# Weight conversions, block sums and one eviction placed elsewhere in the order of a fused attention and MLP kernel

## The chip, the cores and the metric

The kernel runs on one core of a Trainium2 chip. Five engines work side by side, each on its own list of instructions in order: PE (TensorE, matmul), DVE (VectorE), ACT (ScalarE), POOL (GpSimd) and SP (SyncE, which here only issues DMAs). The metric is the device time of one execution in microseconds (us). The kernel before takes 791.88 us, the median of five runs (791.40 to 792.34).

## The reference

Two blocks follow each other. The first is a cross attention between 512 tokens and 32 states, for 8 batches of 8 heads of width 64, read in both directions. The second is an MLP whose hidden layer is multiplied by its own cosine.

```python
scores = scale * np.matmul(x, state.transpose(0, 1, 3, 2))
a = softmax(scores)            # max taken off, sum + 1e-09
xread = np.matmul(a, state)
scores2 = scale * np.matmul(state, x.transpose(0, 1, 3, 2))
a2 = softmax(scores2)
sread = np.matmul(a2, x)
attn_out = np.concatenate([xread, sread], axis=2)
...
x = attn_out.transpose(0, 2, 1, 3).reshape(B * S, H * D)   # 8 x (512 + 32) rows of 512
h = x @ w_in                   # 512 x 2048
g = h * np.cos(h)
return g @ w_out               # 2048 x 512
```

The attention's inputs are float32. `w_in` and `w_out` are float64, so the kernel turns them into float32 from their bits.

## The kernel before, in words

**Steps and tiles.** The order of all instructions is written out by hand. The kernel walks through 144 tiles, one for each step of the loop at L838: 16 tiles for each of the 8 batches (one for each 128 of the 2048 hidden columns), and 16 more for the state rows. A step belongs to one tile t. `hidden(t)` (L466) computes the 128x512 pre-activation h on PE, from the attention weights `aT` and the product `sw` of the states with `w_in`. The gate then goes `gate` (L475, ACT: add a large number to round), `gate2` (L478, DVE: subtract), `gate3` (L483 and L484, ACT: Abs, then Sin) and `gate4` (L490, DVE: multiply by h, write a slot of `g_all`). There are two PSUM buffers for h, so the h of a tile waits for gate4 of the tile two before it.

**Output.** `output(t)` (L609) multiplies a finished tile with `w_out` on PE (L534). It comes three tiles later (`LAG`), four in the first 16 steps, at the end of a step. Batches are taken in pairs with a seven product scheme after Strassen, over the four blocks a11, a12, a21, a22 of `w_out`. A tile has a phase: 0 and 1 are the halves of the first batch of the pair, 2 and 3 those of the second. Phase 0 uses a11, phase 1 a12, phase 2 the block sum s1, phase 3 the sums s4 and s2. What is left over of a pair (`p7` with s3, `p4` with a22) is done while the next pair runs (`more`, L515). In phases 2 and 3 `sums` and `sums2` take differences of tiles (L496); in the first pair all of them on POOL.

**Block sums.** `blocks` (L822) computes half of a block sum in one POOL instruction (L823, 128x1024), at the step that `block_at` (L826) gives: s1 = a21 + a22, s2 = s1 - a11, s4 = a12 - s2, s3 = a11 - a21, where s3 overwrites a21.

**Weights.** 18 loads of float64 weights (L166) are fetched into three raw areas inside `g_all`. Loads 4, 5, 7, 8, 10 and 11 are parts of `w_in` from its second 512 columns on; 6 and 9 are a11, 12 and 13 a12, 14 and 16 a22, 15 and 17 a21. `convert(i, parts)` (L205) turns load i into float32 in six operations: "1" (L224) and "2" (L227) on ACT, "a", "b" and "c" (L231, L233, L236) on DVE, "d" (L241) on POOL. Part "f" fetches load i + 3 into the raw area that is now free, on SP's queue (L194). `conv_at` (L818) gives the step of "1" and "2"; the other parts come one step later. "2" writes one of two scratch areas by turns, which "d" reads.

**Attention of the next batch.** The batch after the current one is prepared between the steps, by the plan at L747: `tokens` and `scores` on PE, `max1`, `spread1`, `shift`, `max2`, `sums` and `norm1` on DVE, `exps` on ACT, then `turn` and `reads` on PE, and the four `products` of states and `w_in` (L316), each with an eviction to `sw` (L443) by ACT (`products_kept`) or DVE (`products_taken`). After the second `reads` of a batch the x of the next one is loaded on SP's queue (L289, L109, L112). In step 6 `states_kept` (L148, DVE) evicts the second half of the transposed states. `warm` (L708) issues matmuls whose result nobody uses.

**Inside a step** the order is: `hidden`, PE's parts of the plan, `gate`, `gate2`, the first parts of ACT and DVE, the parts "a" to "f" of the last conversion, "1" of the present one (or after gate4, where ACT has a first part), `gate3`, `gate4`, `sums`, the second parts, "2", the block sum, `sums2` and `output`. In step 3 four warm matmuls and the products of batch 0's second 512 columns are put in by hand, with their eviction, ahead of the first parts.

Of the kernel before, what the change touches and what calls it, by code (L numbers as in the profile page):

```python
# [12 lines left out]
ALU = mybir.AluOpType  # L13
# [10 lines left out]
def kernel(  # L24
# [47 lines left out]
    a11, a12 = w_out[:, 0, 0:NH], w_out[:, 0, NH:NF]  # L72
    a21, a22 = w_out[:, 1, 0:NH], w_out[:, 1, NH:NF]
    s1 = consts.tile([P, NH, HD], F32)
    s2 = consts.tile([P, NH, HD], F32)
    s3 = a21
    s4 = consts.tile([P, NH, HD], F32)
# [26 lines left out]
    def load_x(b):  # L104

        src = x[b].rearrange("h (c p) d -> p c h d", p=P)
        if b < 2:
            for h in range(H):
                nc.sync.dma_start(out=x_b[:, :, h], in_=src[:, :, h])  # L109
        else:  # L110
            for c in range(NC):
                nc.sync.dma_start(out=x_b[:, c], in_=src[:, c])  # L112
# [27 lines left out]
    def states(half, to):  # L140
        for i in range(4):
            nc.tensor.transpose(out=to[:, P * i:P * i + P],
                                in_=st[:, 4 * half + i, :], identity=ident)

    def states_kept(half, to):
        dst = slice(4 * half, 4 * half + 4)
        src = to.rearrange("p (b m) -> p b m", b=4)
        nc.vector.tensor_scalar(stT[:, dst], src, 1.0 / TWO_PI, None,  # L148
                                op0=ALU.mult)
# [30 lines left out]
    def fetch(n):  # L180
        nonlocal n_fetched
        while n_fetched < n:
            dst, src = loads[n_fetched]
            if f64:
                m, w = dst.shape[1:]

                at_, c0 = (n_fetched - 2) % 3, 0
                if n_fetched < 4:
                    at_, c0 = n_fetched // 2, n_fetched % 2 * 2 * m * w
                if n_fetched >= N_LOADS:  # L190
                    at_ = 3 + n_fetched - N_LOADS
                raw = raw_at[at_].bitcast(I32)[:, c0:c0 + 2 * m * w]
                raw = raw.rearrange("p (m f) -> p m f", m=m)
                nc.sync.dma_start(out=raw, in_=src.bitcast(I32))  # L194
                raws[n_fetched] = raw.rearrange("p m (f w) -> p m f w", w=2)
            else:
                nc.sync.dma_start(out=dst, in_=src)
            n_fetched += 1
# [6 lines left out]
    def convert(i, parts):  # L205

        for p in parts:  # L210
            if p == "f":
                if i not in (1, 2) and i + 3 < N_LOADS:
                    fetch(max(i + 4, 6))
            elif f64:
                convert_part(i, p)
# [32 lines left out]
    class Attention:  # L248
# [126 lines left out]
        def sums(self):  # L375
            self.reduce1([self.z1[:, j] for j in range(2)], ALU.add)
            self.inverse(self.m1 if self.b == 0 else self.i12)
# [73 lines left out]
    def part(b, name, *args):  # L451

        if b not in attn:
            attn[b] = Attention(b)
        getattr(attn[b], name)(*args)
        if (name, args) == ("reads", (1,)) and b + 1 < B:
            if b > 0:
                attn[b + 1] = Attention(b + 1)
                attn[b + 1].load_tokens()
            load_x(b + 1)  # L460
# [5 lines left out]
    def hidden(t):  # L466
        t.hp = hps.tile([P, S], F32, name="h")[:, 0:t.n]
        for i in range(t.kn):
            nc.tensor.matmul(out=t.hp, lhsT=t.lhs(i), rhs=t.rhs(i),  # L469
                             start=(i == 0), stop=(i == t.kn - 1))  # L470

    def gate(t):

        t.q = msb.tile([P, S], F32, name="q")[:, 0:t.n]
        nc.scalar.activation(t.q, t.hp, func=ACTF.Copy, bias=MAGIC)  # L475

    def gate2(t):
        nc.vector.scalar_tensor_tensor(out=t.q, in0=t.q, scalar=MAGIC,  # L478
                                       in1=t.hp, op0=ALU.subtract,
                                       op1=ALU.subtract)  # L480

    def gate3(t):
        nc.scalar.activation(t.q, t.q, func=ACTF.Abs)  # L483
        nc.scalar.activation(t.q, t.q, func=ACTF.Sin, bias=halfpi,  # L484
                             scale=-TWO_PI)

    def gate4(t):
        t.slot = g_free.pop(0)
        t.g = g_all[:, t.slot, 0:t.n]
        nc.vector.tensor_tensor(t.g, t.hp, t.q, op=ALU.mult)  # L490
# [7 lines left out]
    MAIN, SIDE = 0, 1  # L498
# [85 lines left out]
    def sums2(t):  # L584
        pr, i = t.pair, t.i
        if t.phase == 3:
            minus(pr, pr.b[1, i].g, pr.b[1, i].g, pr.b[0, i].g)
# [120 lines left out]
    def warm(n, to):  # L708

        for _ in range(n):  # L710
            nc.tensor.matmul(out=to, lhsT=zeros[:, 0:P], rhs=zeros, start=True,
                             stop=True)
# [34 lines left out]
    def plan(b):  # L747
# [68 lines left out]


    conv_at = {s: 4 + i for i, s in enumerate(  # L818
        (0, 1, 2, 3, 4, 5, 6, 7, 8, 10, 11, 12, 13, 14))}
    conv_at.update({B * NF + 5: N_LOADS, B * NF + 7: N_LOADS + 1})  # L820

    def blocks(op, out_, a, b, r):  # L822
        nc.gpsimd.tensor_tensor(out_[:, r], a[:, r], b[:, r], op=op)  # L823

    lo, hi = slice(0, NH // 2), slice(NH // 2, NH)
    block_at = {15: (ALU.add, s1, a21, a22, lo),  # L826
                17: (ALU.add, s1, a21, a22, hi),
                18: (ALU.subtract, s2, s1, a11, lo),
                19: (ALU.subtract, s2, s1, a11, hi),
                20: (ALU.subtract, s4, a12, s2, lo),  # L830
                21: (ALU.subtract, s4, a12, s2, hi),
                22: (ALU.subtract, s3, a11, a21, lo),
                23: (ALU.subtract, s3, a11, a21, hi)}
    LAG = 3

    line = []
# [1 line left out]
    for step, t in enumerate(all_tiles):  # L838
        s = step % NF
        if s == 0 and t.b < B:  # L840
            steps = plan(t.b)
        todo = [p[s] if t.b < B else [] for p in steps]

        def go(n):
            for p in todo[n]:
                part(*p)

        last, conv = conv_at.get(step - 1, -1), conv_at.get(step, -1)
        if step == B * NF + (0 if f64 else 8):
            fetch(N_LOADS + 2)  # L850
        if step == 4:
            warm(1, acc[MAIN][0])
        if step != 1:
            hidden(t)
        if step == 0:
            hidden(all_tiles[1])
            warm(3, acc[MAIN][0])
            gate(t)
            gate2(t)
            convert(3, "bcdf")  # L860
            convert(4, "1a")
            go(0)
        else:
            go(0)
            if step == 5:
                states(1, acc[SIDE][1])
            gate(t)
            gate2(t)
            if step == 3:
                warm(4, acc[MAIN][0])  # L870
                part(0, "products", 1, SIDE)
                part(0, "products_kept", 1, SIDE)
            go(1)
            go(3)
            if step == 1:
                convert(4, "bcdf")
            elif last >= 0:
                convert(last, "abcdf")
            if conv >= 0 and not todo[1]:
                convert(conv, "1")  # L880
        gate3(t)
        if later:
            later.pop(0)()
        gate4(t)
        if conv >= 0 and todo[1] and step > 0:
            convert(conv, "1")
        if t.pair is not None:
            sums(t)
        if step == 6:
            states_kept(1, acc[SIDE][1])  # L890
        go(2)
        if conv >= 0:
            convert(conv, "2")
        go(4)
        if step in block_at:
            blocks(*block_at[step])
        if t.pair is not None:
            sums2(t)
        while len(line) >= (LAG if step >= 2 * NH else LAG + 1):
            output(line.pop(0))  # L900
        line.append(t)
# [32 lines left out]
```

## Time and profile before

| | before |
|---|---|
| median of 5 runs | 791.88 us |
| the profiled execution's own time | 791.40 us |
| its span, first to last instruction | 789.6 us |
| PE busy | 766.6 us (97%), 2664 matmuls |
| DVE busy | 431.0 us (55%) |
| ACT busy | 390.3 us (49%) |
| POOL busy | 178.7 us (23%) |
| PE o L534, all forms (with `w_out`, with sums) | 236.4 and 177.3 us |
| PE h L469 (512 wide) | 241.6 us |
| POOL g_all L496 | 112.1 us, 80 times, 1422 ns each |
| POOL L241 on w_out | 23.9 us, 10 times, 2393 ns each |
| mean granted TensorE clock | 0.999 |

A page of the profile gives busy times by engine and by group of instructions; a group is a source line, an engine, and what it writes and reads (`o<-g_all,w_out`). A wait is put down to the engine and line that released it last. In the timeline a row has its start and its duration in us, engine, line, operation, output and inputs with shapes, and, in square brackets, how long the engine stood before it and what released it. A duration includes the end of an instruction that the next one on the same engine overlaps, so the distance from start to start is somewhat shorter than the duration. All instructions before about 200 us belong to the first pair of batches, with the weight conversions in its first 17 steps.

### The profile page before, as it was taken

Reading aid. Unit: us, or ns where it says so; the run is one execution under the profiler, and the core shown is the slowest. Engines: PE = TensorE matmul, PEld = TensorE weight load, DVE = VectorE, ACT = ScalarE, POOL = GpSimd, SP = SyncE. Lnnn points to the kernel's source line nnn. Section 1 sums busy time; section 2 is a strip of 40 time slices with the busy share of each in tenths; the row PEclk is TensorE's granted clock in tenths of the full one; section 3 lists DMA queues with packets and bytes.
Section 4 is the critical chain, followed back from the end, with each engine's and each line's share of the span. In section 5 each row is a group of like instructions: output and inputs, shape, how many; then the busy total and the mean of one; then the engine's idle time right before and its main releaser. Section 6 shows DMA issues by size and latency. Waiting matters only on the chain.

```text
span 789.6 us, 7555 instructions
## 1 busy us (share of the span) xinstructions
PE 766.6 (97%) x2664; PEld 340.4 (43%) x2664; DVE 431.0 (55%) x675; ACT 390.3 (49%) x626; POOL 178.7 (23%) x119
## 2 busy tenths in 40 slices
PE   8998899899999999999999999999999999999997
PEld 4442333344344344444444434434444444455554
DVE  5879887732564467744554467635553545431531
ACT  3877964644364445643473436443563445322222
POOL 3343359684000000451000000740000004610200
PEclk9999999999999999999999999999999999999999
DMA  8484361041010610150003410340100114000021
GB/s 239 160 244 182 126 141 28 0 88 20 0 27 13 107 27 14 30 104 0 15 14 54 80 27 6 53 76 0 27 1 0 27 27 117 17 0 15 14 41 40
DMA packets 161958, 43.49 MB, mean 55 GB/s; under 512 B 153921, under 2 KB 153921, under 8 KB 161921
## 3 DMA queue, kind: packets, MB, share of 16 engines
q1 hardware_dynamic: 161024, 42.49, 24.6%
q10 hardware_dynamic: 768, 0.39, 0.2%
q8 instruction: 21, 0.34, 0.2%
q0 software_dynamic: 128, 0.13, 0.1%
q14 instruction: 17, 0.13, 0.1%
HBM read 34.08 MB, written 8.91 MB: 54 GB/s over the span
## 4 chain that ended last, share of the span: by engine, by line
PE 80%; ACT 9%; DVE 8%; issue 1%; DMA 1%; POOL 1%; SPq 0%; ACTq 0%; DVEq 0%; POOLq 0%
PE o L534 44%; PE h L469 26%; PE at L316 4%; PE o L654 3%; PE at L406 2%; DVE q L478 1%; ACT q L483 1%; ACT q L484 1%; DVE g_all L490 1%; ACT s L227 1%; ACT q L475 1%; DVE xT L336 1%; ACT xT L362 1%; DVE aT L383 1%; PE o L316 1%
## 5 line engine op out<-in xcount | busy, mean ns | idle before, releaser
L469 PE MATMUL h<-aT,sw 128*128 128x512 f32 x512 | 241.6, 594 | 12.5 <-DVE g_all L490 10.3
L534 PE MATMUL o<-g_all,w_out 128*128 128x512 f32 x512 | 236.4, 598 | 1.2 <-POOL w_out L241 1.2
L496 POOL TENSOR_TENSOR g_all<-g_all 128x512 f32<-128x512 f32 x80 | 112.1, 1422 | 450.8 <-DVE g_all L490 447.2
L475 ACT ACTIVATE q<-h 128x512 f32<-128x512 f32 (+1 forms) x144 | 82.3, 571 | 261.0 <-PE h L469 260.9
L478 DVE SCALAR_TENSOR_TENSOR q<-q,h 128x512 f32<-128x512 f32 (+1 forms) x144 | 94.2, 654 | 207.2 <-ACT q L475 207.1
L534 PE MATMUL o<-g_all,s 128*128 128x512 f32 x384 | 177.3, 598 | 0.0
L490 DVE TENSOR_TENSOR g_all<-h,q 128x512 f32<-128x512 f32 (+1 forms) x144 | 94.8, 658 | 124.4 <-ACT q L484 118.2
L469 PEld LDWEIGHTS h<-aT,sw 128*128 128x128 f32 x512 | 96.3, 190 | 137.4 <-issue 109.2
L534 PEld LDWEIGHTS o<-g_all,w_out 128*128 128x128 f32 x512 | 94.0, 190 | 125.5 <-issue 118.4
L483 ACT ACTIVATE q<-q 128x512 f32<-128x512 f32 (+1 forms) x144 | 87.8, 610 | 96.3 <-DVE q L478 96.3
L534 PEld LDWEIGHTS o<-g_all,s 128*128 128x128 f32 x384 | 70.8, 190 | 91.7 <-issue 87.3
L484 ACT ACTIVATE q<-q,halfpi 128x512 f32<-128x512 f32 (+1 forms) x144 | 100.9, 700 | 4.5
L241 POOL TENSOR_TENSOR w_out<-w_out,s 128x1024 int32<-128x1024 int32 x10 | 23.9, 2393 | 79.5 <-DVE w_out L236 79.5
L496 DVE TENSOR_TENSOR g_all<-g_all 128x512 f32<-128x512 f32 x48 | 33.2, 692 | 1.6
L443 ACT COPY sw<-at 128x512 f32<-128x512 f32 x50 | 26.8, 590 | 9.0 <-PE at L316 9.0
L469 PE MATMUL h<-sT,w_in 128*128 128x256 f32 x128 | 30.2, 379 | 0.0
L654 PE MATMUL o<-w_out,g_all 128*128 128x512 f32 x64 | 29.6, 592 | 0.0
L469 PEld LDWEIGHTS h<-sT,w_in 128*128 128x128 f32 x128 | 24.3, 190 | 10.1 <-issue 6.2
L316 PE MATMUL at<-w_in,stT 64*32 64x512 f32 x400 | 27.2, 601 | 0.0
L241 POOL TENSOR_TENSOR w_in<-w_in,s 128x1024 int32<-128x1024 int32 (+1 forms) x10 | 19.6, 1964 | 32.1 <-DVE w_in L236 18.5
L540 DVE SCALAR_TENSOR_TENSOR held<-o,held 128x512 f32<-128x512 f32 x40 | 25.3, 676 | 2.3 <-PE o L534 2.3
L561 DVE STREAM_TRANSPOSE ot<-held 128x512 f32<-128x512 f32 x32 | 22.2, 692 | 0.0
(83 smaller groups left out, 445.0 us busy)
## 6 DMA issues: line engine op xcount, KB each, us to landing
out_dram<-ot SPq DMA_DIRECT2D x132, 64.0 KB, 2.0
g_all<-in_moe_w_out_dram SPq DMA_DIRECT2D x8, 1024.0 KB, 4.9
g_all<-in_moe_w_in_dram SPq DMA_DIRECT2D x6, 1024.0 KB, 5.2
xT<-in_x_dram SPq DMA_DIRECT2D x96, 64.0 KB, 2.3
x_b<-in_x_dram SPq DMA_DIRECT2D x24, 256.0 KB, 4.7
x_b<-in_x_dram SPq DMA_DIRECT2D x16, 128.0 KB, 4.0
g_all<-in_moe_w_in_dram SPq DMA_DIRECT2D x4, 512.0 KB, 6.0
x_b<-in_moe_w_out_dram SPq DMA_DIRECT2D x1, 1024.0 KB, 5.9
```

What stands on the lines that cost most here:

```text
L241: nc.gpsimd.tensor_tensor(bits, bits, e.bitcast(I32), op=ALU.add)
L316: nc.tensor.matmul(out=(to or at)[j][Ns * k:Ns * k + Ns, 0:n], lhsT=w[D * j:D * j + D, self.b, Ns * k:Ns * k + Ns], rhs=r(slice(D * j, D * ...
L443: (copy or nc.scalar.copy)(sw_of[self.b, nt][:, j, c0:c1], to[j][:, 0:c1 - c0])
L469: nc.tensor.matmul(out=t.hp, lhsT=t.lhs(i), rhs=t.rhs(i), start=(i == 0), stop=(i == t.kn - 1))
L475: nc.scalar.activation(t.q, t.hp, func=ACTF.Copy, bias=MAGIC)
L478: nc.vector.scalar_tensor_tensor(out=t.q, in0=t.q, scalar=MAGIC, in1=t.hp, op0=ALU.subtract, op1=ALU.subtract)
L483: nc.scalar.activation(t.q, t.q, func=ACTF.Abs)
L484: nc.scalar.activation(t.q, t.q, func=ACTF.Sin, bias=halfpi, scale=-TWO_PI)
L490: nc.vector.tensor_tensor(t.g, t.hp, t.q, op=ALU.mult)
L496: engine.tensor_tensor(out, a, b, op=ALU.subtract)
L534: nc.tensor.matmul(out=acc[bank][ch], lhsT=w[:, i, P * ch:P * ch + P], rhs=g.g, start=(i == 0), stop=(i == NH - 1))
L654: nc.tensor.matmul(out=acc[MAIN][i], lhsT=t.g[:, P * i:P * i + P], rhs=w_out[:, :, t.f, :], start=(t.n_th == 0), stop=(t.n_th == NF - 1))
```

## The change

Three places in the hand-written order change; the operations themselves, their number and their sizes stay as they are.

Conversions 10 to 17 go to later steps: 10 from step 6 to 7, 11 from 7 to 8, 12 from 8 to 10, 13 from 10 to 11, 14 from 11 to 12, 15 from 12 to 13, 16 from 13 to 14, 17 from 14 to 15. Their DVE and POOL parts and their fetches follow one step behind, as before. Steps without "1" and "2" are now 6 and 9 (9 and 15 before).

The six halves of s1, s2 and s4 go one step later each, and the two of s3 from steps 22 and 23 to 32 and 33, which are the first two of the second pair.

The ACT eviction of the products in step 3 goes from before the first parts to behind `gate3`, that is behind that step's conversion part "1", Abs and Sin.

```diff
     conv_at = {s: 4 + i for i, s in enumerate(
-        (0, 1, 2, 3, 4, 5, 6, 7, 8, 10, 11, 12, 13, 14))}
+        (0, 1, 2, 3, 4, 5, 7, 8, 10, 11, 12, 13, 14, 15))}
...
-    block_at = {15: (ALU.add, s1, a21, a22, lo),
-                17: (ALU.add, s1, a21, a22, hi),
-                18: (ALU.subtract, s2, s1, a11, lo),
-                19: (ALU.subtract, s2, s1, a11, hi),
-                20: (ALU.subtract, s4, a12, s2, lo),
-                21: (ALU.subtract, s4, a12, s2, hi),
-                22: (ALU.subtract, s3, a11, a21, lo),
-                23: (ALU.subtract, s3, a11, a21, hi)}
+    block_at = {16: (ALU.add, s1, a21, a22, lo),
+                18: (ALU.add, s1, a21, a22, hi),
+                19: (ALU.subtract, s2, s1, a11, lo),
+                20: (ALU.subtract, s2, s1, a11, hi),
+                21: (ALU.subtract, s4, a12, s2, lo),
+                22: (ALU.subtract, s4, a12, s2, hi),
+                32: (ALU.subtract, s3, a11, a21, lo),
+                33: (ALU.subtract, s3, a11, a21, hi)}
...
             if step == 3:
                 warm(4, acc[MAIN][0])
                 part(0, "products", 1, SIDE)
-                part(0, "products_kept", 1, SIDE)
             go(1)
             go(3)
...
         gate3(t)
+        if step == 3:
+            part(0, "products_kept", 1, SIDE)
         if later:
             later.pop(0)()
         gate4(t)
```

## The prediction

> **What bounds the kernel now.** I read the engine shares first (PE busy 766.6 of 789.6 us), then the waits of PE, then the order of time around them. The waits of PE from 35 to 200 us (us in total, times, longest):
>
> ```profile
> PE h L469 <- DVE g_all L490: 8.4, 6, 2.7
> PE h L469 <- ACT sw L443: 1.7, 1, 1.7
> PE o L534 <- POOL w_out L241: 1.2, 1, 1.2
> PE o L316 <- DVE stT L148: 1.1, 1, 1.1
> PE at L271 <- ACT xT L280: 0.5, 1, 0.5
> PE o L316 <- POOL w_in L241: 0.2, 1, 0.2
> ```
>
> That is 13.1 us; from 200 us to the end there is one row:
>
> ```profile
> PE h L469 <- DVE g_all L490: 1.4, 2, 0.7
> ```
>
> PE's list of instructions is the same in both kernels, so the time can change by what becomes of these waits, and by the PE clock (granted 1.00 in every stretch I asked for). The last waits before 200 us end at 107.39 (step 16), 150.56 and 156.12 (steps 26 and 27). From 107.39 to 148 PE runs without a wait. So I follow the change step by step to the point where PE closes up, and ask how late that is. I write h(t), gate(t), gate4(t), o(t) for tile t's L469, L475, L490 and L534.
>
> **Part 1, the copies of step 3.** The timeline there, ACT and PE:
>
> ```profile
> 42.60 1.07 ACT L443 COPY sw<-o 128x512 f32<-128x512 f32 x2 [3.06 <-PE o L316]
> 43.56 1.17 ACT L224 ACTIVATE w_in<-g_all 128x1024 f32<-128x1024 f32 x1
> 44.63 0.62 ACT L483 ACTIVATE q<-q 128x512 f32<-128x512 f32 x1
> 45.28 0.72 ACT L484 ACTIVATE q<-q,halfpi 128x512 f32<-128x512 f32 x1
> 46.92 0.58 ACT L475 ACTIVATE q<-h 128x512 f32<-128x512 f32 x1
> ```
>
> ACT stands 3.06 us for PE, and then does L224, Abs, Sin and L227 behind the copies. Placed after Sin, the copies leave L224 (1.09 from start to next start), Abs (0.66) and Sin (0.63) to run from 39.45 (behind gate(3)) inside that wait: L224 to 40.54, Sin done 41.84. The load that L224 reads was issued at 33.07 and lands in 5.2 (median of that form), 38.3. The copies still start at 42.60, since PE sets them; L227 follows at 43.56 and ends 44.63; gate(4) then waits for h(4) alone: h starts 43.45, and gate follows an unhindered h by 1.91 (113.97 to 115.88), so 45.36. Gain at gate(4): 46.92 - 45.36 = 1.56. If the load landed after 41 the gain would shrink one for one; its bounds are 0 and 1.56.
>
> PE does not gain at once: o(0) waits for POOL's L241 until 46.63 in either kernel. Followed through ACT and DVE with the same spacings: gate(5) 50.36 (51.71 before; now h(5) sets it), gate(6) 55.62 (56.91), stT's L148 at 60.12 (61.43), and PE's products in step 7, which wait for it, 1.31 earlier.
>
> **Part 2, the conversions.** Eight move (10 to 17; 12 by two steps), so step 6 loses L224 and L227 (2.2 us of ACT), step 7 the three DVE operations L231, L233, L236 (0.72 + 0.72 + 1.24 = 2.7) and L241 on POOL (2.36); the same are added in steps 15 (ACT) and 16 (DVE, POOL). What is taken out of steps 6 and 7 buys little: ACT in step 7 waits for PE's products anyway (copies at 62.02), then has Abs, Sin, L224, L227 in a row, and gate(8) comes at 66.46 (67.78 before, 1.32 earlier). DVE, no longer held by L236, takes L478 of step 8 0.62 behind it, 67.08 instead of 68.58: 1.50. From there to step 11 the chain is DVE and ACT as before, 1.52 earlier.
>
> The cost is at conversion 12 (first half of a12), which o(8) reads at the end of step 12. Before, L241 finished it at 79.64 + 2.36 = 82.00; after, it takes the place that conversion 13 has now:
>
> ```profile
> 89.46 1.88 PE L534 MATMUL o<-g_all,w_out 128*128 128x512 f32 x4
> 91.06 2.36 POOL L241 TENSOR_TENSOR w_out<-w_out,s 128x1024 int32<-128x1024 int32 x1 [9.05 <-DVE w_out L236]
> 91.57 1.98 PE L469 MATMUL h<-aT,sw 128*128 128x512 f32 x4 [0.23 <-DVE g_all L490]
> ```
>
> That L241 then runs 89.54 to 91.90, and o(8), which PE reaches at 89.46 - 1.52 = 87.94, starts at 91.95: a new wait of 4.0 us. Behind it in PE's queue stand h(13), the products and reads of step 13, o(9); for h(13) waits gate(13) on ACT. From 91.95 PE has no slack left. With the spacings of before: o(8) 1.82, h(13) 1.81, products 1.02, reads 1.03, o(9) 1.82, h(14) 1.81, reads 1.02, o(10) 1.82, h(15) 1.72, o(11) 1.72, h(16) 1.82, keep2 and products 1.22, o(12) and o(13) 3.54; sum 22.17, so h(17) at 114.12 against 113.97. The waits of 2.67, 1.70 and 0.89 earlier are moved rather than removed, and 0.23 and 1.79 are swallowed. Net so far **+0.15 us**.
>
> Does another engine undercut this? gate(15) = 104.10 + 1.91 = 106.01, later than the 105.40 of before, but gate2(15) is set by DVE (gate4(14) at 106.2, then 106.8). In step 15 L231 starts under POOL's L241 (106.3 to 108.7); at 107.84 before such an L231 took 1.82 instead of 0.69. I carry it to the end of L241 + 0.5: L236 ends 111.2, gate4(15) 111.2 (111.57). Step 16: gate2 111.8, copies to 113.6, the added three to 116.3, gate4(16) 116.3 (114.31 before, 2.0 later); h(18) needs it by 117.55 and could start at 117.05: covered by 0.5; without cover it would cost one for one.
>
> POOL then has L241 116.45 to 118.8, tile 16's L496 to 120.1, and the first half of s1 to 122.5. Before:
>
> ```profile
> 114.12 2.35 POOL L823 TENSOR_TENSOR s<-w_out 128x1024 f32<-128x1024 f32 x1
> 116.44 1.27 POOL L496 TENSOR_TENSOR g_all<-g_all 128x512 f32<-128x512 f32 x1
> 122.55 1.02 PE L534 MATMUL o<-g_all,s 128*128 128x512 f32 x2
> ```
>
> The first row ended at 116.47, six us before PE wanted it (o(16), 122.55). After, PE wants it at 122.70 and it is there at 122.5: 0.2 us of slack. A slip of 1 us in POOL costs 0.8.
>
> The fetches go with the conversions, one step later each. Load 17, issued at 96.02 before, goes at 99.5 and lands in 5.1, 104.6; its L224 starts at 106.5. In SP's queue it now stands ahead of the xT loads of batch 2, which wait for the reads of step 14 (102.0 instead of 100.3) and end 1.7 later, 111.8; first used at 120.55. Hidden; the cover is 6 us.
>
> **Part 3, the block sums.** s1, s2, s4 one step later, each read three or more steps on; behind the s1 above they keep pace (3.63 us of POOL in a 3.4 to 4.6 us step). s3 leaves steps 22 and 23 (140.33 and 144.68, 2.36 each) for POOL's place behind tile 31's L496, which is empty after 189.7. It is first read by o(32)'s companion at the end of step 35, near 204. Cost 0. Gain: the waits of 1.88 and 0.98 at h(26) and h(27) follow gate(24), an ACT chain of Exp and table loads, and norm1 (L383, 2.11 beside POOL's L496 of tile 24, 1.21 in step 11). POOL is idle from 147.05 to 150.64, so it is not s3 that holds them. I take 0; the bounds are 0 and -2.9.
>
> The Trainium skill, "SBUF — State Buffer" (SBUF: two separate sides), says a GpSimd operation and a DVE operation in a two-port mode, or with two SBUF inputs, exclude each other for a whole instruction. By that rule s3 beside L348 (0.73 instead of 0.17 at 141.97) is a real conflict, of half a us, and the rows agree; but the s4 half that now falls there would hold L348 as well.
>
> **The PE clock.** The longest wait of PE between 35 and 200 us is 2.67 us, and the clock stayed at 1.00. The new one is 4.0 us. A slow clock is seen only at the start: the first four L711 took 1057 ns, the later twenty 592, and L271 groups of four shrink from 1.06 to 0.63 us near 7 us. So 5.5 us at 0.56 of the speed, a loss of 2.4 us: the upper bound of what 4.0 us of standing could cost; the lower is 0. I take 0, as 2.67 cost nothing.
>
> The Trainium skill, "TensorE: Matmul & The Clock Gate" (HAM oscillation), speaks against this change: no PE gaps above some 3.4 us, else the clock halves for a window. By it, as an estimate, 1.7 us would be lost in the executions in which the free-running window falls inside the gap; the trace of before shows no such gap.
>
> **Sum.** Against the profiled execution's own 791.40 us (span 789.6 and 1.8 around it): 791.40 + 0.15 = 791.55. The median of the five runs is 0.48 higher, so **792.0 us**. A measurement of this kernel tells no change from 0.2% or more, 1.6 us.
>
> **Rivals.**
> - *The lead of step 3 is not there* (late load, or the copies held by something else). Then L241 ends at 93.42, o(8) starts 1.5 later, all of it on PE: 0.15 + 1.5, 793.7, slower. For: PE is without slack from o(8) on. Against: the load has 1.1 us to spare.
> - *The clock drops in the 4.0 us wait*: 0.15 + 2.4, 794.5, slower. It decides once the standing is longer than the clock bears, somewhere above 2.67.
> - *Steps 22 to 27 get free of POOL* and the waits of 1.88 and 0.98 go: 0.15 - 2.86, 789.3, faster. For: L383's 2.11. Against: the idle POOL above.
> - *o(8) is not held*, PE keeps the 1.5 lead, and s1 holds o(16) by 0.3: 790.8, no change by the bound. Against: the order of POOL's L241.
>
> **How the numbers follow.** My forecast 0.56 (its own range, from the 0.5 and 0.2 us of slack that might fail and a lead of up to 1, 791.0 to 793.1); step 3 fails 0.13; clock 0.13; steps 22 to 27 0.13; o(8) free 0.05. Faster: 0.13 and 0.02 of the last, 0.15. Slower: 0.13 and 0.13, and 0.03 from the forecast's upper end, 0.29. No change 0.56. The range leaves out the case at 789.3 and a little on each side, under 0.2: 790.4 to 794.6.
>
> **What would show it.** gate(4) 1.5 us earlier; a wait of PE for L241 of about 4 us at o(8), near 92; the wait at h(16) gone; gate4(16) some 2 us later without a wait at h(18); s1's first half ending just before o(16); waits of 1.9 and 1.0 at h(26), h(27) as now. A clock below 1.00 near 90 us, a wait for L823 at o(16) of over a us, or waits at h(26) and h(27) under half as long would make the forecast wrong.

## The result, and the profile after

The changed kernel takes 794.0 us (median of 24 runs, 793.06 to 794.76), the kernel before 791.74 us (median of 44 runs, 791.25 to 792.8). The ratio is 1.0027 with a 95% interval of 1.0021 to 1.0032: slower by 0.27%, and by 2.3 us between the medians. The time lies inside the range of the prediction, on the side of the rival with the clock, and not at the forecast of 792.0; it is above the forecast's own range, which ended at 793.1. The profiled execution took 793.27 us, with a span of 791.5.

The waits of PE from 35 to 200 us after the change (us in total, times, longest):

```profile
PE h L469 <- DVE g_all L490: 6.1, 4, 2.7
PE o L534 <- POOL w_out L241: 5.0, 2, 3.8
PE o L316 <- DVE stT L148: 0.4, 1, 0.4
PE o L316 <- POOL w_in L241: 0.2, 1, 0.2
```

They sum to 11.7 us, 1.4 less than before, and yet the kernel is longer. The wait at h(16) (1.79) is gone, the one for the copies in step 11 (1.7) too, and a wait of 3.8 us for POOL's L241 is new. The timeline shows where it is (start, duration, and in brackets the time the engine stood):

```profile
89.47 2.35 POOL L241 TENSOR_TENSOR w_out<-w_out,s 128x1024 int32<-128x1024 int32 x1 [9.04 <-DVE w_out L236]
...
91.88 2.92 PE L534 MATMUL o<-g_all,w_out 128*128 128x512 f32 x4 [3.82 <-POOL w_out L241]
...
94.58 2.69 PE L469 MATMUL h<-aT,sw 128*128 128x512 f32 x4
...
115.63 1.88 PE L469 MATMUL h<-aT,sw 128*128 128x512 f32 x4
```

This is o(8), which waits for conversion 12, then h(13), and, last, h(17). The reader should look at the durations: o(8) takes 2.92 us and h(13) 2.69 us. The same two rows took 1.88 and 1.98 us before. The wait alone can't do that; the clock can. Stretches of 5 us follow: the window and its length, the busy us of PE, PE's weight loads, DVE, ACT and POOL with the number of instructions in brackets, then the granted clock (1.00 is full speed), DMA share and GB/s; first the kernel before, then the changed one:

```profile
90.00:95.00 5.00, 4.77 (x34) 1.63 (x34) 4.93 (x7) 4.41 (x7) 2.36 (x1) 1.00 0.54 180
95.00:100.00 5.00, 5.00 (x36) 2.63 (x32) 4.22 (x6) 4.97 (x9) 2.37 (x1) 1.00 0.68 216
```

```profile
90.00:95.00 5.00, 3.12 (x5) 1.50 (x6) 4.89 (x6) 4.40 (x7) 2.32 (x2) 0.78 0.63 213
95.00:100.00 5.00, 5.00 (x38) 2.05 (x37) 1.99 (x4) 2.31 (x5) 1.86 (x1) 0.88 0.55 210
```

A mean clock of 0.78 and 0.88 over two times 5 us is 0.22 x 5 + 0.12 x 5 = 1.7 us of full clock not granted, just where PE has no slack, and the others wait for it (ACT is busy for 2.31 us in the second stretch instead of 4.97). h(17), the tile at which PE closes up, starts at 115.63; in the forecast it was 114.12, and before 113.97:

```profile
113.97 1.88 PE L469 MATMUL h<-aT,sw 128*128 128x512 f32 x4
```

### The profile page after: what moved, and what is told of

It is laid out like the page before. It is cut to its first block, busy times and chain, and to the rows that moved or that the text cites. A ratio compares the mean times of both kernels' runs of the same rounds, so it can differ in the third digit from the quotient of the medians.

```text
span 791.5 us, 7554 instructions
## 1 busy us (share of the span) xinstructions
PE 769.7 (97%) x2664; PEld 341.3 (43%) x2664; DVE 430.2 (54%) x675; ACT 390.8 (49%) x626; POOL 178.6 (23%) x119
## 4 chain that ended last, share of the span: by engine, by line
PE 82%; DVE 8%; ACT 6%; issue 1%; DMA 1%; POOL 1%; SPq 0%; ACTq 0%; DVEq 0%; POOLq 0%
PE o L534 45%; PE h L469 27%; PE at L316 4%; PE o L654 3%; PE at L406 2%; DVE q L478 1%; DVE g_all L490 1%; DVE xT L336 1%; ACT q L483 1%; ACT xT L362 1%; DVE aT L383 1%; ACT q L475 1%; ACT q L484 1%; PE o L316 1%; ACT aT L357 1%
## 5 line engine op out<-in xcount | busy, mean ns | idle before, releaser
L241 POOL TENSOR_TENSOR w_out<-w_out,s 128x1024 int32<-128x1024 int32 x10 | 23.9, 2388 | 81.2 <-DVE w_out L236 76.8
L469 PEld LDWEIGHTS h<-sT,w_in 128*128 128x128 f32 x128 | 24.3, 190 | 10.1 <-issue 6.2
L241 POOL TENSOR_TENSOR w_in<-w_in,s 128x1024 int32<-128x1024 int32 (+1 forms) x10 | 19.7, 1965 | 36.7 <-DVE w_in L236 25.8
```

The lines of the kernel that those rows point to most:

```text
L241: nc.gpsimd.tensor_tensor(bits, bits, e.bitcast(I32), op=ALU.add)
L469: nc.tensor.matmul(out=t.hp, lhsT=t.lhs(i), rhs=t.rhs(i), start=(i == 0), stop=(i == t.kn - 1))
```

## The experiments

Each was run against the kernel before on the same chip, in five rounds. The ratios are to the kernel before on that chip, whose median was 791.50, 791.59 and 791.70 us on the three chips used.

**Four unused matmuls in the wait.** PE works through the wait; o(8) starts no earlier.

```diff
+        if step == 12:
+            warm(4, acc[SIDE][0])
         while len(line) >= (LAG if step >= 2 * NH else LAG + 1):
             output(line.pop(0))
```

> The changed kernel with four matmuls whose result nobody uses (3.4 us by the rows of L711) put in front of o(8) in step 12, so that PE works through the wait for conversion 12. Clock theory (the loss beyond the forecast is the half clock that follows the 3.82 us of standing): no slow stretch behind o(8), h(17) near 114.1 instead of 115.63, time 1.5 us below the changed kernel, about 792.3. Rival (the wait itself and what stands behind it cost the 2.2 us, the clock is a bystander): 794.0, unchanged, since o(8) starts no earlier.

791.33 us (791.02 to 792.92), ratio 1.0001 (0.9992 to 1.001): 2.7 us less than the changed kernel by the medians (2.4 when each is counted from the kernel before that it was run with), and no longer distinguishable from the kernel before. The expectation had said 1.5 us less. The timeline (this execution is 0.4 us later from its start on):

```profile
88.30 3.60 PE L711 MATMUL o<-g_all 128*128 128x512 f32 x8
89.88 2.37 POOL L241 TENSOR_TENSOR w_out<-w_out,s 128x1024 int32<-128x1024 int32 x1 [9.03 <-DVE w_out L236]
92.30 1.98 PE L534 MATMUL o<-g_all,w_out 128*128 128x512 f32 x4 [0.40 <-POOL w_out L241]
94.12 1.88 PE L469 MATMUL h<-aT,sw 128*128 128x512 f32 x4
...
114.36 1.88 PE L469 MATMUL h<-aT,sw 128*128 128x512 f32 x4
```

The four L711 replace 3.4 of the 3.8 us of standing, o(8) still starts as soon as L241 is done, and o(8) and h(13) are back at 1.98 and 1.88 us. From o(8) to h(17) PE takes 22.06 us, where the changed kernel took 23.75. The stretches say the same:

```profile
90.00:95.00 5.00, 4.60 (x12) 1.84 (x11) 4.93 (x7) 4.42 (x8) 2.32 (x2) 1.00 0.60 213
95.00:100.00 5.00, 5.00 (x40) 2.26 (x39) 3.65 (x6) 3.99 (x7) 2.31 (x1) 1.00 0.67 210
```

So added work made the changed kernel faster. The loss beyond the wait was the clock, and the rival explanation falls. It isn't the profiled execution alone: the mean granted clock of a whole run is 0.991 to 0.996 in all runs of the changed kernel, and 0.995 to 0.999 in the eleven with the four matmuls (slow stretches that cost no time, as at h(11), count in it too).

**Two unused matmuls.** The same edit with `warm(2, ...)`.

> The changed kernel with two of the unused matmuls (1.7 us) in front of o(8) instead of four, so that PE still stands some 2.1 us before o(8). Clock theory: a stand of 2.1 us is too short to empty the window, or seldom enough, so most of the gain of the four stays: 791.3 to 792.0. Rival (any stand before o(8) costs in proportion): half way between 791.3 and 794.0, about 792.7.

791.68 us, 791.11 to 794.12, ratio 1.0005 (0.9996 to 1.0014). The median is where the clock theory put it, but 4 of the 11 runs are above 792.7: a stand of 2.1 us (the trace shows 2.11) seems to be followed by the slow clock now and then. The profiled execution has the clock at 1.00 from 85 to 105 us, so no trace shows what those four runs lost. Their mean granted clocks over the whole run speak for the clock: 0.992 to 0.996 in the four, 0.998 to 1.000 in the other seven.

**Matmuls in front of h(11) as well.** Four in front of o(8), and `warm(3, acc[SIDE][0])` ahead of `hidden` in step 11, where both kernels stand for 2.67 us.

> The changed kernel with the four matmuls in front of o(8) and three more (2.6 us) in front of h(11), where PE stands 2.67 us in both kernels and where the profile of the changed kernel shows the first slow stretch of the clock (from 79.1 us). Clock theory: no slow stretch at all, 791.1 to 791.4 and less spread than with the four alone (791.02 to 792.92). Rival (slow stretches come at random, whatever PE does): the same spread as with the four alone.

791.62 us (790.99 to 792.3), ratio 0.9998 (0.9989 to 1.0007). The profiled execution has no slow stretch between the start and the end (granted clock 0.999). The time didn't fall to the expected 791.1 to 791.4, and the spread shrank only from 1.9 to 1.3 us. Part of what remains comes from elsewhere: this profiled execution of 792.25 us is 0.5 us behind the one with four matmuls at h(10) already (73.08 against 72.62). So the wait at h(11) is not what costs time.

**The eviction alone.** The kernel before, with `products_kept` of step 3 behind `gate3`, and nothing else.

```diff
-                part(0, "products_kept", 1, SIDE)
...
         gate3(t)
+        if step == 3:
+            part(0, "products_kept", 1, SIDE)
```

> The kernel before with only the eviction of step 3 moved behind Sin. Theory (its lead of 1.5 us at gate(4) passes down to step 16, where PE closes up): 1.5 us faster, 790.2. Rival (the lead is eaten by a wait between step 4 and 16, or PE's clock drops in a wait that has grown): 791.7, no change.

789.94 us (789.75 to 790.3), ratio 0.9979 (0.997 to 0.9988): 1.56 us faster, as the theory had it. The timeline of ACT in steps 3 and 4:

```profile
42.70 1.07 ACT L443 COPY sw<-o 128x512 f32<-128x512 f32 x2 [0.76 <-PE o L316]
...
43.65 1.18 ACT L227 ACTIVATE s<-g_all 128x1024 f32<-128x1024 uint32 x1
45.45 0.60 ACT L475 ACTIVATE q<-h 128x512 f32<-128x512 f32 x1 [0.62 <-PE h L469]
```

The copies stand where they did, but only 0.76 us of ACT's 3.06 us of standing are left in front of them, and gate(4) comes at 45.45 instead of 46.92. PE's waits of 2.67, 1.68 and 1.77 us at h(11), h(12) and h(16) are all still there; the whole chain just lies 1.4 us earlier. This is the fastest kernel of the study: it beats both.

**Without the eviction.** The changed kernel with `products_kept` of step 3 back in its old place.

> The changed kernel with the eviction of step 3 back in its old place: conversions and sums alone. Theory: conversion 12 ends 1.5 us later at 93.4, PE reaches o(8) 1.5 later too, the wait and the clock drop stay, so 794.0 + 1.5 = 795.5. Rival (the lead of step 3 is worth nothing once the wait at o(8) sets the pace): 794.0.

795.8 us (795.39 to 796.72, five runs), ratio 1.0055 (1.0042 to 1.0067). The theory's 795.5 holds. o(8) and h(17), and the stretches of this profile:

```profile
93.57 3.78 PE L534 MATMUL o<-g_all,w_out 128*128 128x512 f32 x4 [3.84 <-POOL w_out L241]
...
118.24 1.88 PE L469 MATMUL h<-aT,sw 128*128 128x512 f32 x4
```

```profile
90.00:95.00 5.00, 1.43 (x2) 0.83 (x3) 4.93 (x7) 4.41 (x7) 2.35 (x1) 0.70 0.49 177
95.00:100.00 5.00, 5.00 (x15) 1.70 (x21) 1.66 (x2) 1.87 (x4) 2.35 (x1) 0.61 0.61 201
```

Here 0.30 x 5 + 0.39 x 5 = 3.45 us were not granted, twice the 1.7 us of the changed kernel's profile. In stretches of half a us the slow clock is 0.50 there, for some 3.4 us in that execution and for twice as long in this one (from 92.0 to 98.9 us). Not all of it costs time: here it begins 1.5 us before o(8), while PE still stands. From o(8) to h(17) PE takes 24.67 us, 2.6 more than the 22.06 at full clock; in the changed kernel's profile it was 1.7 more.

**Without the eviction, with four unused matmuls.**

> Conversions and sums later, the eviction of step 3 in its old place, and the four unused matmuls in front of o(8). Theory (three terms that add: lead of step 3 -1.6, wait at o(8) +1.5, clock +2.4 to +2.7): before + 1.5 = 793.0 to 793.3, below the 795.8 without the four matmuls. Rival (the wait at o(8) without the lead costs more than PE's standing, the matmuls help less): over 794.

792.86 us (792.71 to 793.89), ratio 1.0018 (1.0009 to 1.0027), 2.9 us below the 795.8 without the matmuls (3.1 counted from the kernel before each); granted clock 0.999.

```profile
93.39 1.98 PE L534 MATMUL o<-g_all,w_out 128*128 128x512 f32 x4 [0.41 <-POOL w_out L241]
...
115.45 1.88 PE L469 MATMUL h<-aT,sw 128*128 128x512 f32 x4
```

Here too PE takes 22.06 us from o(8) to h(17). So conversions and sums without clock loss cost 792.86 - 791.70 = 1.2 us (the theory had 1.5, its interval 793.0 to 793.3 is missed by a little).

**The block sums alone.** The kernel before with the new `block_at`.

> The kernel before with only the block sums later. Theory: nothing waits for POOL at any of the places, 791.5 to 791.8, no change. Rival (s3 off POOL in steps 22 and 23 frees DVE and the waits at h(26) and h(27)): 788.9 to 790.

791.63 us (791.28 to 792.39), ratio 1.0 (0.9991 to 1.0009). Nothing gained, nothing lost; that s3 on POOL holds up steps 22 to 27 is refuted.

**Eviction and block sums.**

> The kernel before with the eviction moved and the sums later, conversions untouched. Theory (the sums are worth nothing): 789.9, as the eviction alone. Rival (with PE earlier, s1 one step later holds o(16) or POOL holds DVE): over 790.5.

790.34 us (789.93 to 791.41), ratio 0.9986 (0.9977 to 0.9995). It lies between the two expectations, and its interval overlaps that of the eviction alone, so the two can't be told apart.

**Conversion 12 one step earlier.** The changed kernel with conversion 12 in step 9.

```diff
-        (0, 1, 2, 3, 4, 5, 7, 8, 10, 11, 12, 13, 14, 15))}
+        (0, 1, 2, 3, 4, 5, 7, 8, 9, 11, 12, 13, 14, 15))}
```

> The changed kernel with conversion 12 in step 9 instead of 10. The wait at o(8) goes. Theory (all of the loss hangs on that wait and the clock behind it): PE keeps its lead until the first half of s1 holds it, time 790.5 to 791.2, below the kernel before. Rival (the later conversions 13 to 17 and the sums load steps 13 to 19 and cost by themselves): 792.5 or more.

792.66 us (792.05 to 793.68), ratio 1.0013 (1.0005 to 1.0022): a miss for the theory, and the rival's number came. The wait at o(8) is gone, but PE's waits for gate4 are 10.1 us, against 6.1 in the changed kernel and 8.4 before:

```profile
PE h L469 <- DVE g_all L490: 10.1, 7, 2.7
PE o L534 <- POOL w_out L241: 1.2, 1, 1.2
```

Step 9 has the next batch's Exp on ACT. With conversion 12 there, L227 comes in front of gate(10), which starts at 80.17 instead of 78.97 in the changed kernel, and the three DVE operations come in front of gate4(10), which starts at 85.77 instead of 83.19; h(12) then waits 1.22 us, and h(16) 2.45. Both kernels leave step 9 without "1" and "2"; this run doesn't. The rival's reason, the later 13 to 17, is not what holds h(16) here: it starts at 107.95, and in the last experiment below, where 13 to 17 come in the same steps as here and 10 to 12 earlier, at 105.52.

**Conversions 13 to 17 only.** The eviction moved, 12 in its old step 8, 13 to 17 in steps 11 to 15, the first half of s1 in step 15, and the other sums as changed.

```diff
-        (0, 1, 2, 3, 4, 5, 6, 7, 8, 10, 11, 12, 13, 14))}
+        (0, 1, 2, 3, 4, 5, 6, 7, 8, 11, 12, 13, 14, 15))}
...
     block_at = {15: (ALU.add, s1, a21, a22, lo),
-                17: (ALU.add, s1, a21, a22, hi),
+                18: (ALU.add, s1, a21, a22, hi),
...
```

> The kernel before with the eviction moved, and with only conversions 13 to 17 one step later, so that 12 keeps its place ahead of o(8) and step 10, where ACT has Exp's table loads, is free of a conversion; the first half of s1 stays in step 15, which needs loads 14 and 15 alone, the other sums as in the changed kernel. Theory (the harm of the change is conversion 12 alone): no wait at o(8), the wait of 1.77 at h(16) shrinks or goes, 788.2 to 789.5, below the 789.94 of the eviction alone. Rival (what leaves step 10 comes back in steps 15 and 16): 789.9 or more.

791.82 us, ratio 1.0008 (0.9999 to 1.0017): another miss, and the rival is right. The runs fall in two groups, 791.59 to 791.82 (six) and 792.89 to 793.61 (five); what sets them apart is open. The mean clock doesn't: it is 0.995 to 0.998 in the faster six and 0.993 to 0.997 in the slower five. There is no wait at o(8), but the wait at h(16) has grown to 2.06 us, since PE comes there 0.7 us earlier than in the run of the eviction alone, and gate4(14) only 0.5. In this profile a slow stretch of the clock begins there (h(16) takes 2.97 us, and the mean clock from 105 to 110 us is 0.66). In step 16, the added operations meet the sum on POOL, which this edit left in step 15:

```profile
112.25 2.79 POOL L823 TENSOR_TENSOR s<-w_out 128x1024 f32<-128x1024 f32 x1
112.88 2.72 DVE L233 TENSOR_SCALAR w_out<-w_out 128x1024 int32<-128x1024 int32 x1
...
116.96 0.69 DVE L490 TENSOR_TENSOR g_all<-h,q 128x512 f32<-128x512 f32 x1
...
117.71 1.98 PE L469 MATMUL h<-aT,sw 128*128 128x512 f32 x4 [0.39 <-DVE g_all L490]
```

L233 takes 2.72 us beside L823, where it takes 0.69 alone, gate4(16) slips to 116.96 (112.89 in the run of the eviction alone), and h(18) waits 0.39 us for it. That sets the time of this profile: h(18) is 1.72 us later than with the eviction alone (115.99), and the two profiled executions are 1.82 us apart (791.74 and 789.92). The slow stretch before it is hidden, since DVE runs from gate4(14) to gate4(16) without a wait.

## Why the prediction was right or wrong

**The copies of step 3: right.** gate(4) was to come at 45.36, and came at 45.57 in the changed kernel. Alone, the part is worth 1.56 us against 1.5.

```profile
39.60 1.16 ACT L224 ACTIVATE w_in<-g_all 128x1024 f32<-128x1024 f32 x1
...
40.64 0.64 ACT L483 ACTIVATE q<-q 128x512 f32<-128x512 f32 x1
41.31 0.72 ACT L484 ACTIVATE q<-q,halfpi 128x512 f32<-128x512 f32 x1
...
42.81 1.08 ACT L443 COPY sw<-o 128x512 f32<-128x512 f32 x2 [0.77 <-PE o L316]
...
45.57 0.60 ACT L475 ACTIVATE q<-h 128x512 f32<-128x512 f32 x1 [0.63 <-PE h L469]
```

These are ACT's rows of the changed kernel: L224, Abs and Sin run inside the old wait, and gate(4) follows at 45.57.

**The conversions as far as o(8): right.** L241 of conversion 12 was forecast for 89.54 and started at 89.47; o(8) was forecast for 91.95 and started at 91.88; the wait was to be 4.0 us and was 3.82.

**Sum without the clock: right.** +0.15 us was forecast. With the wait filled by matmuls, the time is 791.33 against 791.50, which the interval doesn't tell from zero.

**The PE clock: the step that failed.** The prediction took 0 from its bounds of 0 and 2.4 us, "as 2.67 cost nothing". By its own signs that makes the forecast wrong: it named a clock below 1.00 near 90 us, and the clock from 90 to 95 us was 0.78. The stand of 3.82 us did cost: the profile shows 1.7 us not granted, and filling the stand gives back 2.4 to 2.7 us in the medians with the eviction and 2.9 to 3.1 without it. The upper bound, made from the slow start of PE (5.5 us at 0.56 of the speed), was about right for one execution: the two profiles with the stand lost 1.7 and 2.6 us of PE's time. That executions with the longer slow stretch make the medians' loss larger than the changed kernel's one profile shows is likely, not shown.

The row of 2.67 us could not bear the step, for two reasons. It was the longest wait that the prediction had between 35 and 200 us, and 4.0 us lies past it. And it came from one execution: in 7 of the 11 profiles with that wait the clock does fall behind it (last section), and the time doesn't change because PE has another wait to lose it in. Behind o(8) there is none, as the prediction itself said ("no slack left").

The rule of the Trainium skill that the prediction weighed and set aside, in "TensorE: Matmul & The Clock Gate" (HAM oscillation), was the better guide here: this case's rows now agree with it at 3.82 us. They don't agree with its limit of some 3.4 us: the clock fell behind stands of 2.67 us too.

**Steps 15 to 19: right in kind.** gate4(16) slipped, h(18) had no wait, and s1 became available at the last moment. The forecast had 0.2 us of slack, and almost none is left:

```profile
120.66 1.26 POOL L496 TENSOR_TENSOR g_all<-g_all 128x512 f32<-128x512 f32 x1
121.89 2.36 POOL L823 TENSOR_TENSOR s<-w_out 128x1024 f32<-128x1024 f32 x1
```

L823 ends at 124.25, and o(16) starts at 124.30, right behind h(19). The slow clock did not use the slack up. With the four matmuls, at full clock, the same rows leave 0.06 us:

```profile
120.61 2.36 POOL L823 TENSOR_TENSOR s<-w_out 128x1024 f32<-128x1024 f32 x1
...
123.03 1.98 PE L534 MATMUL o<-g_all,s 128*128 128x512 f32 x4
```

**Block sums: right.** Alone they change nothing, and in the changed kernel the waits at h(26) and h(27) are 1.88 and 0.97, as before (1.88 and 0.98).

**Rivals.** The clock rival came true, priced at 2.4 us against 2.4 to 2.7. Its total of 794.5, like those of the first and third rival, has the +0.15 twice, since 792.0 holds it already: 794.4, 793.5 and 789.2 would be the sums. That the time lies inside the stated range is owed to this rival, for whose sake the range was drawn up to 794.6, and not to the path that was forecast. "Step 3 fails" and "steps 22 to 27 get free" are refuted by the runs of one part alone. That o(8) is not held is refuted by the profile.

Together, each counted from the kernel before that it was run with: the eviction alone gives -1.6 us; conversions and sums without clock loss cost 1.2 us; the clock costs 2.4 us with the eviction and 3.1 without. The sum is 2.0 to 2.7 us; measured were 2.3.

## What to carry to other kernels

Where work is moved behind a deadline, look for the consumer's standing time and not only for the delay: if the array has slack, a wait of some us may cost nothing by itself and still bring down the clock for the dense work that follows. A few matmuls without use in front of the consumer, sized to end with the wait, test that in one run. Look at the clock in several executions, since one can have the slow stretch and the next not. And a row that shows a wait of one length to be harmless says nothing on a longer one, nor on the same wait where no slack follows.

## What the runs showed of the hardware that was not expected

A stand of 2.67 us at h(11) is followed by the slow clock in some executions and not in others. Eleven profiles have that wait unfilled: the two kernels and every experiment but the one with matmuls in front of h(11). In seven of them (the changed kernel, four and two unused matmuls, conversion 12 earlier, block sums alone, eviction and block sums, conversions 13 to 17) h(11) lasts 2.5 to 3.7 us instead of 1.98, and the mean clock from 80 to 85 us is 0.66 to 0.78; in the other four it stays at 1.00. The changed kernel's stretches:

```profile
75.00:80.00 5.00, 2.32 (x6) 0.74 (x5) 3.83 (x7) 4.97 (x9) 1.92 (x1) 0.91 0.37 99
80.00:85.00 5.00, 5.00 (x23) 1.19 (x21) 3.86 (x8) 4.97 (x7) 0.43 (x1) 0.75 0.48 187
```

It costs little there, because PE has a later wait (1.7 us at h(12) before) in which the lost time disappears: that wait is gone from the changed kernel's list, and its PE is no later for it (h(12) starts at 85.20, and with the eviction alone, at full clock, at 85.38). The 1.7 us at h(12) stand in all five profiles with h(11) at full clock and in none of the seven.

Shorter stands differ as well: one of 2.06 us at h(16) was followed by the slow clock (conversions 13 to 17), one of 2.11 at o(8) and one of 2.45 at h(16) were not (two unused matmuls, conversion 12 earlier). What decides between the two outcomes at the same length of wait is open; no run varied it by itself.
